# A second transform level on 64x32 and 32x64 tiles, eight in turn, in an attention and long-convolution kernel

## The chip, the cores and the metric

The kernel runs on one core of one Trainium2 chip, as one launch. TensorE (PE, with its weight loads as PEld), VectorE (DVE), ScalarE (ACT), GpSimd (POOL) and SyncE (SP) each work through a queue of their own, in order; DMA transfers run beside them on 16 DMA engines. The metric is the device time in microseconds (us). Before the change three runs took 217.52, 217.57 and 216.03 us, the median being 217.52.

## The reference

Two independent computations stand side by side in the output, 2048 positions by 2 x 576 columns, everything in bfloat16.

Half A is a sliding attention with 32 heads of 18 columns. Each position looks at 8 keys at distances 0, 2, ..., 14:

```python
qkv = (x @ wqkv).reshape(B, S, 3, H, Dh)          # H = 32, Dh = 18
idx = pos[:, None] - (jnp.arange(8) * 2)[None, :]
logits = einsum("bhsd,bhswd->bhsw", q, kg) * scale   # masked where idx < 0
o = einsum("bhsw,bhswd->bhsd", softmax(logits), vg)
a = o.reshape(B, S, D) @ wo
```

Half B is a gated long convolution. A four-tap filter along the positions, a product, a convolution as long as the sequence (by FFT in the reference), a direct term and another product:

```python
k_shift = sum(k_pad[:, t:t + S, :] * shift_k[:, 3 - t] for t in range(4))
kv = k_shift * v
y = irfft(rfft(kv, 2 * S) * rfft(ssm_k, 2 * S))[:S]
b = q * (y + kv * ssm_D)
```

## The kernel before

**The order** of all work is written out by hand in the string `ORDER` (lines 18 to 47). Each word names a step, its indices and, behind a colon, which PSUM pool it uses (`a` or `b`, two buffers of two banks each), which engine evacuates PSUM (`s` ScalarE, `v` VectorE) and which queue issues its DMAs (`c` ScalarE's; none means SyncE's). The loop at line 666 calls the steps in this order, and each engine's queue holds its instructions in it. Before the change no word has a `c`: every DMA is issued by SP. `MAP` (line 50) places all buffers in one arena of SBUF by hand, many of them sharing space one after another.

**DMA semaphores.** Eight of them go round in the order of issue, over all queues. A DMA therefore waits, in the queue that issues it, for the landing of the DMA eight issues earlier, and what stands behind it in that queue waits with it.

**Half A.** `xt` (line 364) loads x transposed by a DMA transpose, sixteen pieces in all; `xl4` and `x4` bring the last 64 columns. `qk` and `qt` (lines 391, 399) project queries and keys, `qt` those of the last 64 columns with weights that `wt` gathers; `v` (line 373) projects values. `lm` (line 495) multiplies queries by shifted keys on VectorE, `lb` (line 506) sums over the columns of a head on TensorE, `sm` (line 530) is the softmax. `pm` (line 598) multiplies values by weights, again on VectorE, 18 times; `ps` (line 604) sums over the eight keys. `po` (line 616) is the output projection: 72 matmuls on 32x128 tiles, two evacuations, and here one store per evacuation.

**Half B.** `lkn` loads the filter, `kt` and `kp` (lines 475, 485) transpose it and take the first transform level; `cv` (line 452) is the four-tap filter and the product with v, 32 VectorE operations; `sx` (line 464) takes the first level of kv. Both write the first level's result to scratch in DRAM (`Dk`, `Dx`), because the second level needs it with other indices on the partitions. `kl` and `xl` read it back, `ks` and `xs` do the second level through the helper `s2` (line 552), `gp` (line 575) multiplies the two spectra on VectorE, `gi` (line 583) is the inverse of the second level and writes to scratch `Dy`; `yl` reads that back, `ql` loads q, and `ys` (line 640) does the inverse of the first level, multiplies by q and stores. The second level's index runs over 32 blocks, four to a load (`i` from 0 to 7).

In `s2` a partition carries two interleaved residues. The weights `W2` hold, for each block, 64 columns in two halves, one for each residue; `tw` (line 345) makes them from the table `C2` by masks with zeros, so that a matmul with all 128 rows and 64 columns does both residues, half of it with zero weights. Two such tiles fill the array. `g_inv` uses 64 rows and 128 columns, also two tiles, with a table `IAt` that `ia` (line 410) makes from `W2` by transposes.

`evac` (line 117) is the copy from PSUM that most steps use, so most of ScalarE's work stands at line 119 and VectorE's copies at lines 121, 123 and 125.

Of the kernel before, what the change touches and what calls it, by code (L numbers as in the profile page):

```python
# [10 lines left out]
ALU = mybir.AluOpType  # L11
# [19 lines left out]
cv.3.7 sx.4.2:bs lb.2.0:bs ql.1 v.4:as sx.5.1:bs sx.5.2:bs v.3:as kl.3 sx.6.0:bs lm.3.0.0 lm.0.2.1 sx.6.1:bs v.1:as
kl.6 lb.3.0:bs ql.2 sx.7.0:as sx.6.2:as v.0:bs sx.7.1:as sx.7.2:as lm.0.1.1 lm.2.2.1 v.2:bs vh.0 sm.0.0 sm.0.1
lm.0.0.1 sm.0.2 sm.0.3 sm.0.4 lb.0.1:bs xl.3 v.5:as xl.6 lm.2.0.1 v.8:as lm.2.1.1 lb.2.1:bs vh.1 ks.6.0:as sm.0.5:b
ks.3.0:as ks.3.1:bs lm.1.0.1 lm.1.1.1 lm.3.1.1 kl.2 lb.1.1:av xs.3.0:bs ks.6.1:av xl.5 xs.3.1:bs xs.6.0:as sm.0.6 xl.2
xs.6.1:bs gp.3.0 gp.3.1 xl.4 v.7:as lm.3.0.1 v.6:as ks.2.0:bs xs.5.0:as vh.2 sm.0.7 gp.6.0 gp.6.1 lb.3.1:bs pm.0.2
ks.2.1:as xs.2.0:bv kl.5 pm.0.0 xs.2.1:as kl.4 lwo.3 xs.5.1:bs gi.3.0:as gi.6.0:bs pm.0.6 sm.1.0 gp.2.0 gi.3.1:as
sm.1.1 sm.1.2 ks.5.0:bs gp.2.1 ks.5.1:as sm.1.3 kl.1 ps.0.0:bs gp.5.0 ps.0.2:bs xl.1 xs.4.0:as xs.4.1:bs gi.6.1:as
gp.5.1 ks.4.0:bs ks.4.1:as kl.7 gi.5.0:bs pm.0.7 ps.0.6:as pm.0.1 ps.0.7:as ks.1.0:bv sm.1.4 ks.1.1:av xl.7 xs.1.0:bs
kl.0 gp.4.0 gi.5.1:as gp.4.1 gi.2.0:bs gi.2.1:as sm.1.5:b pm.0.4 gp.1.0 ks.7.0:as xs.1.1:bs xl.0 gi.4.0:av sm.1.6
pm.0.5 ql.7 gp.1.1 sm.1.7 gi.4.1:bs ks.7.1:as ps.0.1:bs gi.1.0:as xs.7.0:bs pm.0.3 ks.0.0:as gp.7.0 ps.0.4:bs lwo.2  # L40
gi.1.1:as ks.0.1:bs xs.7.1:av xs.0.0:bs gp.7.1 gp.0.0 xs.0.1:bs gp.0.1 lwo.1 gi.7.0:as gi.7.1:bs gi.0.0:as gi.0.1:bs
yl.3 yl.1 ps.0.5:as yl.2 pm.0.8 ps.0.3:as ps.0.8:bs po.0.1.1:s pm.1.7 pm.1.6 pm.1.1 ps.1.7:as po.0.1.0:s ps.1.1:as
yl.7 pm.1.2 ps.1.2:bs pm.1.5 ys.3.0:b ys.3.1:a po.0.0.1:s pm.1.3 ys.1.0:a ps.1.5:bs ys.1.1:a pm.1.0 yl.5 ps.1.6:bs
yl.6 ql.5 ys.2.0:a ys.2.1:b po.0.0.0:s ql.6 ps.1.0:bs yl.0 pm.1.4 pm.1.8 ps.1.3:bs ys.7.0:a ps.1.4:bs ys.7.1:a
ps.1.8:bs ql.0 ql.4 ys.5.0:b ys.5.1:a po.1.1.1:v yl.4 po.1.1.0:s ys.6.0:a ys.6.1:b ys.0.0:a ys.0.1:b po.1.0.1:v
po.1.0.0:s ys.4.0:a ys.4.1:b
# [4 lines left out]
    "C2": 0, "W2": 0, "c_i": 0, "vt1": 0, "lmask": 2048, "p_i": 2080, "sc_f": 2112, "ones1": 2144, "sc_i": 2272,  # L51
# [651 lines left out]
```

## Time and profile before

| | before |
|---|---|
| three runs | 217.52, 217.57, 216.03 us |
| profiled execution, its own time | 216.0 us |
| its span, first to last instruction | 214.2 us |
| DVE busy | 190.3 us (89%) |
| PE busy, weight loads | 185.7 us (87%), 113.3 us (53%) |
| ACT busy | 155.7 us (73%) |
| mean granted PE clock | 0.969 |
| DMA moved | 50.46 MB, mean 236 GB/s |

A row of a group names the line, the engine, the operation, output and input, the shapes and the count, then the busy time in us and the mean of one in ns, then how long the engine had been idle before such instructions and what ended the wait. A row of the timeline gives the start and the duration in us. `SPq` is SyncE's queue issuing DMAs. A DMA row gives the count, the size of one and the median time from issue to landing.

### The profile page before, as it was taken

To read this page: it belongs to the slowest core of one execution; us is meant where nothing else is said; L and a number is where in the kernel's file an instruction comes from. 1 tells how busy PE (TensorE), PEld (TensorE's weight loads), DVE (VectorE), ACT (ScalarE), POOL (GpSimd) and SP (SyncE) were. 2 spreads that over 40 slices of the span, in tenths; PEclk is the share of its full clock that TensorE was granted. 3 is DMA by queue.
4 is the path that set the end of the run, shared out by engine and by line. 5 is a ranking of instruction groups with operands and counts; after the bars stand their busy time and mean duration, and the time that the engine had idled before them with its cause. 6 is when DMAs were issued, how large, how long until landed. Compare 5 with 4: busy or idle time off the path is not lost.

```text
span 214.2 us, 6277 instructions
## 1 busy us (share of the span) xinstructions
PE 185.7 (87%) x2711; PEld 113.3 (53%) x2711; DVE 190.3 (89%) x174; ACT 155.7 (73%) x229; POOL 6.0 (3%) x24
## 2 busy tenths in 40 slices
PE   7389689999999999999969899879989988988760
PEld 2046345354343335556648567557656866756540
DVE  7777958999999999999999999999999998985432
ACT  3499599998969998887866999899999543340220
POOL 8200000000000000000000000000000000000000
PEclk9956999999999999999999999999999999999997
DMA  6999999999798898985748299767977399698693
GB/s 171 246 203 167 151 335 226 296 187 303 194 293 231 275 265 227 307 297 161 218 123 320 38 271 330 265 231 278 291 195 206 118 274 347 178 343 266 168 329 99
DMA packets 44874, 50.46 MB, mean 236 GB/s; under 512 B 16940, under 2 KB 37998, under 8 KB 44846
## 3 DMA queue, kind: packets, MB, share of 16 engines
q1 hardware_dynamic: 44846, 50.06, 84.3%
q8 instruction: 21, 0.34, 0.7%
q14 instruction: 7, 0.06, 0.1%
HBM read 28.94 MB, written 18.87 MB: 223 GB/s over the span
## 4 chain that ended last, share of the span: by engine, by line
DVE 50%; DMA 16%; PE 11%; issue 10%; SPq 8%; ACT 2%; DVEq 1%; ACTq 0%
DVE arena L500 13%; DVE arena L457 7%; DVE arena L602 7%; DVE arena L460 6%; DMA out_dram<-arena 5%; SPq L366 5%; DMA arena<-in_B_k_dram 5%; DVE arena L577 4%; DMA arena<-in_B_q_dram 3%; DMA arena<-in_B_ssm_k_dram 3%; PE psA L379 2%; ACT arena L119 2%; DVE arena L123 2%; DVE arena L462 2%; PE psB L623 2%
## 5 line engine op out<-in xcount | busy, mean ns | idle before, releaser
L119 ACT ACTIVATE arena<-psA 128x576 bf16<-128x576 f32 (+5 forms) x101 | 73.3, 764 | 32.9 <-PE psB L623 15.0
L119 ACT ACTIVATE arena<-psB 128x576 bf16<-128x576 f32 (+8 forms) x114 | 77.8, 720 | 14.5 <-PE psB L611 6.0
L602 DVE TENSOR_TENSOR arena<-arena 128x4096 bf16<-128x4096 bf16 x18 | 40.5, 2284 | 0.1
L500 DVE TENSOR_TENSOR arena<-arena 128x4096 bf16<-128x4096 bf16 x16 | 36.1, 2284 | 0.0
L371 PE MATMUL psA<-arena 128*128 128x512 bf16 x120 | 27.9, 379 | 2.5 <-DMA arena<-in_A_x_dram 2.0
L371 PEld LDWEIGHTS <-arena 128*128 128x128 bf16 x160 | 15.0, 98 | 20.7 <-issue 4.4
L457 DVE TENSOR_TENSOR arena<-arena 128x2304 bf16<-128x2304 bf16 x16 | 21.5, 1354 | 1.2 <-DMA arena<-in_B_k_dram 0.9
L577 DVE TENSOR_TENSOR arena<-arena 128x2304 bf16<-128x2304 bf16 x16 | 21.1, 1350 | 0.0
L557 PEld LDWEIGHTS <-arena 128*64 128x64 bf16 x256 | 13.8, 108 | 12.7 <-issue 11.9
L623 PE MATMUL psA<-arena 32*128 32x288 bf16 x288 | 19.7, 282 | 0.7 <-DVE arena L651 0.7
L623 PE MATMUL psB<-arena 32*128 32x288 bf16 x288 | 19.3, 281 | 1.0 <-issue 0.6
L623 PEld LDWEIGHTS <-arena 32*128 32x128 bf16 x576 | 15.9, 93 | 5.2 <-issue 3.5
L611 PEld LDWEIGHTS <-ident 64*64 64x64 bf16 x576 | 15.1, 106 | 5.4 <-issue 3.3
L379 PEld LDWEIGHTS <-arena 128*32 128x32 bf16 x360 | 14.5, 140 | 5.4 <-issue 1.4
L460 DVE TENSOR_TENSOR arena<-arena 128x2304 bf16<-128x2304 bf16 x12 | 16.3, 1354 | 0.4
L379 PE MATMUL psA<-arena 128*32 128x512 bf16 x280 | 16.2, 381 | 0.1
L590 PEld LDWEIGHTS <-arena 64*128 64x128 bf16 x256 | 12.7, 94 | 5.7 <-issue 2.2
L651 DVE TENSOR_TENSOR arena<-psA,arena 128x576 bf16<-128x576 f32 x10 | 7.4, 753 | 8.3 <-DMA out_dram<-arena 7.6
L557 PE MATMUL psB<-arena 128*64 128x288 bf16 x136 | 12.7, 290 | 1.9 <-DVE arena L125 0.9
L611 PE MATMUL psB<-arena,ident 64*64 64x256 bf16 x384 | 12.5, 271 | 1.7 <-DVE arena L602 1.2
L557 PE MATMUL psA<-arena 128*64 128x288 bf16 x120 | 12.0, 291 | 2.3 <-DVE arena L123 1.3
L590 PE MATMUL psA<-arena 64*128 64x288 bf16 x160 | 11.9, 283 | 0.5 <-DVE arena L125 0.2
(114 smaller groups left out, 195.5 us busy)
## 6 DMA issues: line engine op xcount, KB each, us to landing
Dk<-arena SPq DMA_DIRECT2D x8, 576.0 KB, 4.2
Dx<-arena SPq DMA_DIRECT2D x8, 576.0 KB, 4.4
arena<-Dk SPq DMA_DIRECT2D x8, 576.0 KB, 4.5
arena<-Dx SPq DMA_DIRECT2D x8, 576.0 KB, 5.2
Dy<-arena SPq DMA_DIRECT2D x8, 576.0 KB, 3.4
arena<-Dy SPq DMA_DIRECT2D x8, 576.0 KB, 4.5
out_dram<-arena SPq DMA_DIRECT2D x32, 144.0 KB, 4.3
arena<-in_A_wo_dram SPq DMA_DIRECT2D x4, 648.0 KB, 6.8
```

What stands on the lines that cost most here:

```text
L119: nc.scalar.activation(dst, src, ACT.Copy, **({} if scale is None else {"scale": scale}))
L371: nc.tensor.matmul(ps[:, u, :], w[:, kb, cols[u]:cols[u] + 128], xT[:, kb, t], start=(kb == 0), stop=(kb == 4))
L379: nc.tensor.matmul(ps[32 * a:32 * a + 32, u, :], wv[:, kb, 2 * n + u:D:DH], xv[kb][:, a], start=(kb == 0), stop=(kb == 4), tile_position=( ...
L457: nc.vector.tensor_tensor(tB() if k else tAr[c], kfull[:, 4 * c + 3 - j:4 * c + 7 - j, :], skb[:, j, :].unsqueeze(1).to_broadcast([128, 4, ...
L460: nc.vector.tensor_tensor(tAr[c], tAr[c], tB(), ALU.add)
L500: nc.vector.tensor_tensor(prr.get((m, h, hv)), qs[hv][h]().unsqueeze(1).to_broadcast([128, 2, 2, HS]), kv, ALU.mult)
L557: nc.tensor.matmul(ps[64 * hp:64 * hp + 64, im, 0:HD], W2[:, im, 4 * i + 2 * h + hp].rearrange("p l f -> p (l f)"), Wt[:, 2 * h + hp, d0:d ...
L577: nc.vector.tensor_tensor(P.rearrange("p (a b) d -> p a b d", a=2), X.unsqueeze(2).to_broadcast([128, 2, 2, D]), K.unsqueeze(1).to_broadca ...
L590: nc.tensor.matmul(ps[:, hp, 0:HD], IAt[r, tab, 2 * i + h, :], Pp[(i, h)][r, n, d0:d1], start=(n == 0), stop=(n == 3), tile_position=(64 * ...
L602: nc.vector.tensor_tensor(Pr.get((hv, p)), vv, Lt[hv]().unsqueeze(2).to_broadcast([128, W, 2, 256]), ALU.mult)
L611: nc.tensor.matmul(ps[64 * b:64 * b + 64, r, 0:256], ident[g, g], P[g, n, :, 128 * b:128 * b + 128], start=(n == 0), stop=(n == W - 1), ti ...
L623: nc.tensor.matmul(pss[e][:, b, 0:HD], Os[hv][g, d // 2, r, 128 * (d % 2):128 * (d % 2) + 128], wo4[g, d, d0:d1], start=(d == 0), stop=(d ...
```

## The change

The weights of the second level hold one residue each, without masks (`C2`, `lmask` and the step `tw` are gone), and a partition carries one residue: the lower 64 one, the upper 64 the other. `s2` takes 16 matmuls of 64 rows and 32 columns in one go, for two row groups and four column groups, on two PSUM buffers at once; its index `e` is a half of the 576 columns. `g_inv` takes 32 matmuls of 32 rows and 64 columns likewise. In both, two row groups write into one PSUM bank, on different partitions. The numbers of matmuls in `s2` and in `g_inv` go from 256 to 512 each.

The scratch `Dk`, `Dx`, `Dy` is laid out so that the first level's side sees 4608 bytes in a row and the second level's side 1152; before it was the other way round.

`po` puts both evacuations into one buffer and stores them by one DMA, eight stores in all where there were sixteen. The load of the first rows of k is cut into 48 and 15 partitions.

`ORDER` and `MAP` are new throughout. Some words now have a `c`: ACT's queue issues the filter loads, two of the sixteen transposes of x, some weight loads, half of the stores of `Dk` and `Dx`, one load from `Dk`, two stores and two loads of `Dy`, and some output stores. Twelve of the sixteen `ys` are evacuated by ScalarE, so that VectorE multiplies from SBUF; before all sixteen multiplied from PSUM.

```diff
-lkn.0 tj lkn.1 t2 t0 wm.11:b ib:bs t3 tv sh zw.1 lkn.2 lk.0 zw.0 sk.2:bv sk.0:bv lwq.0.1 t5 xl4 sk.1:bv xt.0.2 kt.7:av
+t1 sh:c t0 xl4 xt.0.0 lkn.1:c lkn.0:c tj lkn.2:c sk.1:as xt.1.2 t2 lwq.0.1 sk.0:as t3 zw.1 xt.0.3:c xt.1.3 tv sk.2:av
...
-ps.1.8:bs ql.0 ql.4 ys.5.0:b ys.5.1:a po.1.1.1:v yl.4 po.1.1.0:s ys.6.0:a ys.6.1:b ys.0.0:a ys.0.1:b po.1.0.1:v
-po.1.0.0:s ys.4.0:a ys.4.1:b
+ys.7.1:as yl.3 po.0.1.0:s ps.1.2:as ql.2 pm.1.7 yl.0:c ql.0 ys.6.0:av ys.6.1:bs ps.1.7:bs ys.2.0:as ql.3 ys.2.1:bs
+po.1.1.1:s po.1.1.0:v po.1.0.0:s ys.0.0:bv ys.0.1:as ys.3.0:bv ys.3.1:as po.1.0.1:sc
...
     def by_f1(Dd, i):
-        return Dd.rearrange("r f d -> f r d")[:, 4 * i:4 * i + 4, :]
+        return Dd.rearrange("h (q r) d -> (h q) r d", r=32)[:, 4 * i:4 * i + 4, :]
 
     def by_rt(Dd, i):
-        return Dd.rearrange("r (l h) d -> (r l) h d", h=32)[:, 4 * i:4 * i + 4, :]
+        return Dd.rearrange("h p d -> p h d")[:, 4 * i:4 * i + 4, :]
...
-    def t_w2():
-        for l in range(2):
-            evac(W2().rearrange("p i h l f -> p l (i h) f")[:, l], C2(), scale=lmask[:, l:l + 1])
...
-    def s2(Wt, i, dst, h, scale):
-        for e, (d0, d1) in enumerate(DCH):
-            ps = psb()
-            for im in range(2):
-                for hp in range(2):
-                    nc.tensor.matmul(ps[64 * hp:64 * hp + 64, im, 0:HD],
-                                     W2[:, im, 4 * i + 2 * h + hp].rearrange("p l f -> p (l f)"),
-                                     Wt[:, 2 * h + hp, d0:d1], start=True, stop=True, tile_position=(0, 64 * hp))
-            evac(dst[:, :, h, d0:d1], ps[:, :, 0:HD], scale=scale)
+    def s2(Wt, i, dst, e, scale):
+        pss = [psb(), psb()]
+        for im in range(2):
+            for hp in range(2):
+                for l in range(2):
+                    for h in range(2):
+                        o = 64 * (l ^ h) + 32 * hp
+                        nc.tensor.matmul(pss[h][o:o + 32, im, 0:HD], W2[64 * l:64 * l + 64, im, 4 * i + 2 * h + hp, :],
+                                         Wt[64 * l:64 * l + 64, 2 * h + hp, HD * e:HD * e + HD], start=True, stop=True,
+                                         tile_position=(64 * l, o))
+        for h in range(2):
+            evac(dst[:, :, e, HD * h:HD * h + HD], pss[h][:, :, 0:HD], scale=scale)
...
-    def g_inv(i, h):
-        Y = Yr[i] if h else Yr.get(i)
-        for d0, d1 in DCH:
-            ps = psb()
-            for n, tab in enumerate((0, 1, 1, 2)):
-                for hp in range(2):
-                    r = slice(64 * hp, 64 * hp + 64)
-                    nc.tensor.matmul(ps[:, hp, 0:HD], IAt[r, tab, 2 * i + h, :], Pp[(i, h)][r, n, d0:d1],
-                                     start=(n == 0), stop=(n == 3), tile_position=(64 * hp, 0))
-            evac(Y[:, 2 * h:2 * h + 2, d0:d1], ps[:, :, 0:HD])
+    def g_inv(i, e):
+        Y = Yr[i] if e else Yr.get(i)
+        P = Pp[(i, e)]
+        pss = [psb(), psb()]
+        for n, tab in enumerate((0, 1, 1, 2)):
+            for hp in range(2):
+                for b in range(2):
+                    for h in range(2):
+                        r, o = 64 * b + 32 * hp, 64 * (b ^ h)
+                        nc.tensor.matmul(pss[h][o:o + 64, hp, 0:HD], IAt[r:r + 32, tab, 2 * i + h, o:o + 64],
+                                         P[r:r + 32, n, HD * h:HD * h + HD], start=(n == 0), stop=(n == 3), tile_position=(r, o))
+        for h in range(2):
+            evac(Y[:, 2 * h:2 * h + 2, HD * e:HD * e + HD], pss[h][:, :, 0:HD])
...
+        stage = sAr.get((hv, r, di))
         for e in range(2):
-            stage = sAr.get((hv, r, di, e))
-            evac(stage, pss[e][:, :, 0:HD])
-            a = 8 * hv + 2 * (2 * r + e)
-            dq().dma_start(outt[:, a:a + 2, d0:d1], stage)
-            sAr.drop((hv, r, di, e))
+            evac(stage[:, 2 * e:2 * e + 2, :], pss[e][:, :, 0:HD])
+        a = 8 * hv + 4 * r
+        dq().dma_start(outt[:, a:a + 4, d0:d1], stage)
+        sAr.drop((hv, r, di))
```

More of the change, by code (lines that the diff above doesn't have):

```diff
@@ L315, in t_first @@
         nc.vector.tensor_copy(p_f(), p_i[:, 1:2])
-        nc.gpsimd.iota(g1(), pattern=[[4, 64]], base=1, channel_multiplier=0)
+        nc.gpsimd.iota(g1(), pattern=[[4, 32], [128, 2]], base=1, channel_multiplier=0)
         for ri in range(2):
-            nc.vector.tensor_scalar(n1[:, ri, :], g1(), p_f[:, 0:1], 64.0 * (1 + ri), op0=ALU.mult, op1=ALU.add)
+            nc.vector.tensor_scalar(n1[:, :, ri], g1(), p_f[:, 0:1], 64.0 * (1 + ri), op0=ALU.mult, op1=ALU.add)
         nc.vector.tensor_single_scalar(n1(), n1(), 255, ALU.bitwise_and)
-        nc.scalar.activation(T1(), n1(), ACT.Sin, bias=pib[:], scale=-2.0 * np.pi / 256)
+        nc.scalar.activation(T1(), n1().rearrange("p f r -> p (f r)"), ACT.Sin, bias=pib[:], scale=-2.0 * np.pi / 256)
     def t_second():
         nc.gpsimd.iota(g2(), pattern=[[4, 32], [256, 32]], base=0, channel_multiplier=0)
-        for i, bits in enumerate((1, 112, 4, 8, 2)):
+        for i, bits in enumerate((64, 28, 1, 2, 32)):
             nc.vector.tensor_single_scalar(sc_i[:, i:i + 1], p_i[:, 0:1], bits, ALU.bitwise_and)
@@ L339, in t_second @@
         nc.vector.tensor_single_scalar(n2(), n2(), 8191, ALU.bitwise_and)
-        nc.scalar.activation(C2().rearrange("p (i h) f -> p i h f", i=2), n2(), ACT.Sin, bias=pib[:], scale=-2.0 * np.pi / 8192)
+        nc.scalar.activation(W2(), n2(), ACT.Sin, bias=pib[:], scale=-2.0 * np.pi / 8192)
         nc.scalar.preload_act_table_set("natural_log_exp_and_others")
-        nc.vector.tensor_scalar(lmask[:, 0:1], sc_f[:, 0:1], -1.0, 1.0, op0=ALU.mult, op1=ALU.add)
-        nc.vector.tensor_copy(lmask[:, 1:2], sc_f[:, 0:1])
-    def t_w2():
-        for l in range(2):
-            evac(W2().rearrange("p i h l f -> p l (i h) f")[:, l], C2(), scale=lmask[:, l:l + 1])
     def t_heads():
@@ L421, in ib_table @@
         ptr = psum("b", 2, 1024, dt=BF16)
-        nc.tensor.transpose(ptr[:, 0, 0:64], T1[0:64].rearrange("p r f -> p (r f)"), ident[0:64, 0:64])
+        nc.tensor.transpose(ptr[:, 0, 0:64], T1[0:64], ident[0:64, 0:64])
         evac(IB(), ptr[:, 0, 0:64])
```

93 lines of the change are left out of this document (46 added, 47 removed), and 24 rows, old and new, of the table MAP.

## The prediction

> **What bounds the kernel now.** I read the page first, then the busy times by stage, then the timeline of the engine that is full.
>
> ```profile
> span 214.2 us, 6277 instructions
> ...
> PE 185.7 (87%) x2711; PEld 113.3 (53%) x2711; DVE 190.3 (89%) x174; ACT 155.7 (73%) x229; POOL 6.0 (3%) x24
> ...
> DVE 50%; DMA 16%; PE 11%; issue 10%; SPq 8%; ACT 2%; DVEq 1%; ACTq 0%
> ```
>
> DVE and PE look alike by share (89% and 87%), but the chain that ended last is half DVE and only 11% PE. I cut the span where the work of DVE changes: at 34.7 (the convolution runs), 87.7 (its last product), 120, 163.5 (last spectral product) and 190.4 (last attention product, step `pm`).
>
> ```profile
> 0.00:34.70 34.70, 26.09 (x177) 13.71 (x177) 26.12 (x48) 24.66 (x27) 5.66 (x23) 0.85 0.99 209
> 34.70:87.70 53.00, 51.61 (x399) 23.07 (x399) 52.42 (x40) 47.33 (x66) 0.33 (x1) 1.00 0.97 257
> 87.70:120.00 32.30, 29.76 (x473) 19.69 (x477) 32.23 (x23) 25.23 (x37) 0.00 (x0) 1.00 0.69 216
> 120.00:163.50 43.50, 39.74 (x632) 27.31 (x620) 43.43 (x37) 42.39 (x75) 0.00 (x0) 1.00 0.80 245
> 163.50:190.40 26.90, 24.61 (x688) 19.06 (x688) 26.17 (x18) 13.08 (x23) 0.00 (x0) 1.00 0.78 245
> 190.40:214.20 23.80, 13.84 (x352) 10.49 (x352) 9.93 (x15) 2.98 (x5) 0.00 (x0) 0.94 0.77 226
> ```
>
> Columns: stage, its length, busy PE, weight loads, DVE, ACT, POOL, granted PE clock, DMA share, GB/s. From 34.7 to 190.4 DVE is idle for 1.45 us in all. Before that it loses 8.58 us, while the DMA engines are full (0.99). So the span is DVE work up to the last `pm` (190.31 - 9.93 = 180.4), plus idle before it (8.58 + 1.45 = 10.0), plus a tail of 23.8 us in which no engine is full. Those are my three terms. ACT is second in the stage 120 to 163.5 (42.39 of 43.5); PE has 3.8 us to spare there.
>
> **Term 1, DVE work.** The changed program's instructions, counted engine by engine against the old ones, say which evacuations change engine. Prices:
>
> ```profile
> L651 DVE TENSOR_TENSOR arena<-psA,arena 128x576 bf16<-128x576 f32 x10 | 7.4, 753 | 8.3 <-DMA out_dram<-arena 7.6 <-PE psA L646 0.7
> ...
> L123 DVE CAST arena<-psA 128x576 bf16<-128x576 f32 x6 | 4.3, 752 | 0.4 <-issue 0.4
> ...
> L123 DVE CAST arena<-psB 128x1024 bf16<-128x1024 f32 x2 | 2.4, 1220 | 0.4 <-PE psB L448 0.4
> ...
> L123 DVE CAST arena<-psA 128x512 bf16<-128x512 f32 x1 | 0.7, 680 | 0.0
> ...
> L535 DVE TENSOR_TENSOR arena<-arena 128x512 bf16<-128x512 bf16 x2 | 0.8, 420 | 0.0
> ...
> L119 ACT ACTIVATE arena<-psA 128x576 bf16<-128x576 f32 x48 | 29.6, 673 | 21.5 <-PE psB L623 15.0 <-PE psA L623 6.1 <-PE psA L590 0.3
> ...
> L119 ACT ACTIVATE arena<-arena 128x2048 bf16<-128x2048 bf16 x2 | 3.9, 1998 | 0.0
> ```
>
> DVE evacuations of 576 columns fall from 19 to 12: -7 x 0.75 = -5.3. One of 1024 goes, one narrow 1024 and one 512-word copy come (about 0.68 each): +0.2. The tail projections `qt.0` and `qt.1` move to DVE, four 512-column casts of 0.68 and two of 16: +3.1. Twelve of the sixteen `y_step`s now let ACT evacuate and DVE multiply from SBUF; no row has 576 such columns, the 512 row (420 ns) scaled gives 0.45, bounds 0.42 and 0.75: 12 x (0.45 - 0.75) = -3.6. Four one-column table operations go, about -0.6. Sum -6.2: 190.3 becomes 184.1. After the last `pm` stand 5 products, 3 direct ones and 2 casts: 5 x 0.45 + 5 x 0.75 = 6.0, so 178.1 stands ahead of it, against 180.4.
>
> ACT loses the two masked copies of the twiddle table (-4.0) and gains 18 evacuations of 576 columns (12.1), the rest cancelling to about -3: 155.7 becomes some 161. Eight of those us lie in the last two stages, where ACT has 35 us free. In the spectral stage it gets two more steps, 2.4 us against 1.1 free; it can borrow from the stage before (7.1 free).
>
> **The tiles themselves.**
>
> ```profile
> 104.04 0.68 PE L557 MATMUL psA<-arena 128*64 128x288 bf16 x8
> ...
> 159.95 1.15 PE L590 MATMUL psA<-arena 64*128 64x288 bf16 x16
> ...
> 167.43 0.29 PE L623 MATMUL psA<-arena 32*128 32x288 bf16 x1
> ...
> 167.44 0.29 PE L623 MATMUL psB<-arena 32*128 32x288 bf16 x1
> ...
> 167.56 0.28 PE L623 MATMUL psA<-arena 32*128 32x288 bf16 x1
> ```
>
> Today `s2` (L557) and `g_inv` (L590) run two tiles at a time: 8 matmuls in 4 turns, 16 in 8. In L623 four tiles start within 0.01 us and the next four 0.12 us later; so a turn costs 0.12 us and the starts almost nothing. Each of the two steps has 256 matmuls in 128 turns now and 512 in 64 turns after: -128 x 0.12 = -15.4 us of PE. At worst starts fill the array no faster than four at a time, 0 saved. The value for the end is close to 0 either way: DVE is busy for 43.43 of 43.5 us where these steps run, and the two ACT evacuations behind a step (1.2 us) outlast its matmuls. What the new form costs: a step holds both buffers of its PSUM pool and its first evacuation waits for all 16 matmuls, which the other pool covers. I count 0, bounds -1 and +2.
>
> The row first: L623, L590 and L611 give every row group a bank of its own (`pss[e][:, b]`, `ps[:, hp]`). In the changed steps two row groups write one bank, in different partitions. The Trainium skill, page TensorEngine Tiling (Array Packing), section Gotcha 1: PSUM Pressure, says that different row tiles cannot use one PSUM bank at the same time; no row here shows such a pair. It makes the third rival.
>
> **Scratch layout.**
>
> ```profile
> Dk<-arena SPq DMA_DIRECT2D x8, 576.0 KB, 4.2
> arena<-Dk SPq DMA_DIRECT2D x8, 576.0 KB, 4.5
> ...
> Dy<-arena SPq DMA_DIRECT2D x8, 576.0 KB, 3.4
> arena<-Dy SPq DMA_DIRECT2D x8, 576.0 KB, 4.5
> ...
> arena<-in_A_wqkv_dram SPq DMA_DIRECT2D x2, 256.0 KB, 3.4
> ```
>
> Long and short pieces change sides: Dk and Dx are now written in 4608-byte pieces and read in 1152-byte ones, Dy the other way. The old Dk wrote short (4.2), the old Dy long (3.4); both reads take 4.5. Worth -0.8 on the way to the spectra and +0.8 on the way back: 0.
>
> **Term 2, idle before the last `pm`.** The start is built anew, with loads on ACT's queue too.
>
> ```profile
> SPq L366 <- DMA arena<-in_B_ssm_k_dram: 1.9, 1, 1.9
> ...
> L366 SPq DMA_TRANSPOSE arena<-in_A_x_dram x16: 1252/1274/10752, 6.8 to 52.9; - x16
> ...
> DMA to landing us min/median/max: 3.6/4.9/12.2
> ...
> 0.74 1.28 ACT L288 ACT_TABLE_LOAD   x1 [0.74 <-PEq L687]
> ...
> 3.41 0.87 DVE L326 CAST arena<-arena 128x5 f32<-128x5 int32 x1
> ...
> 8.64 2.00 ACT L340 ACTIVATE arena<-arena,pib 128x2048 bf16<-128x2048 int32 x1 [2.15 <-DVE arena L342]
> ```
>
> The first row is the rule of this program: eight DMA semaphores go round, so a DMA waits for the landing of the one eight issues before it, here a transpose for the first filter load. In the new order the second filter load, on ACT, waits so for `xl4` (256 KB; by the 256 KB row about 4.5 us), and behind it stand ACT's table load (1.28) and the first activation, for which L326 waits: 3.41 becomes about 6.2. From L326 to the table's sine took 5.2 us (3.41 to 8.64): sine at 11.4 to 13.4, second table load to 14.7, then the two transposes that are now ACT's (they also wait until SP's have landed), 2 x 1.27, to 17.3. Two evacuations (2 x 1.0), then `lwq.1.1` issued near 20 and landed near 23.7; `wt` 0.75, five matmuls 1.2, so `qt.0` is ready near 26. DVE has 23.2 us of work before the first convolution product in its new order (8.0 of tables, 15.2 of evacuations and `lm.*.2`); `qt.0`, `qt.1` and two `lm` take 5.5 from 26: 31.6, idle 8.4. With 1.6 for later loads I take 10.0 for the start (now 8.58); bounds 6 (all loads in time) and 17 (an ACT transpose that takes 10.75 us to issue, as the first one did). For the rest, 3.0 (now 1.45): 1.3 for ACT in the spectral stage and a little at the first `y_step`s, whose loads come just when five `pm` are done; bounds 1 and 7. Sum 13.0.
>
> Last `pm` at 178.1 + 13.0 = 191.1.
>
> **Term 3, the tail.**
>
> ```profile
> 190.38 1.42 DVE L651 TENSOR_TENSOR arena<-psA,arena 128x576 bf16<-128x576 f32 x2
> ...
> 210.10 1.26 SPq L654 DMA_DIRECT2D out_dram<-arena  x2
> ...
> DVE arena L651 <- DMA out_dram<-arena: 9.4, 4, 3.4
> ...
> 167.42 2.08 PEld L623 LDWEIGHTS <-arena 32*128 32x128 bf16 x72 [0.20 <-issue]
> ...
> 169.74 1.07 PE L611 MATMUL psA<-arena,ident 64*64 64x256 bf16 x32
> ...
> 175.75 0.44 PE L646 MATMUL psB<-arena 128*64 128x288 bf16 x4
> ```
>
> Today nine PE steps of the attention and four `y` pairs follow the last `pm`, and DVE stands 9.4 us for staging buffers still being stored. In the new order one `ps` (1.1), the pairs of tiles 6, 2, 0 and 3, and four `po` follow. On PE: `ps` (L611) 1.1, `ys.2` (two halves, L646) 0.8, three `po` (L623, 72 matmuls) at 2.2, four half `ys` at 0.4, one `po` 2.2, five PSUM handovers of 0.25 = 13.6. Then two evacuations (1.5) and one store, issue and landing 4.4 (the old end had 4.1 from the last product at 210.1 to 214.2): 19.5. Half as many attention stores, 8 for 16, save their issues (0.5 each) on SP, already in this. Bounds 17 and 24 (as now, if stagings wait again).
>
> **Sum.** 191.1 + 19.5 = 210.6, that is -3.6. The profiled execution took 216.0 for its span of 214.2, so 212.4. The three runs shown have 217.52 as median and 216.03 as lowest, so the profiled one is among the low ones; I lift the forecast a little for that: **213.0**.
>
> **Rivals.** (1) *Slower: ACT's queue starves the evacuations.* Eighteen DMAs stand in ACT's queue up to the loads of the spectra, nearly all waiting for a landing eight issues back, with evacuations behind them, and PE has only two buffers a pool. For: in the new order ACT's transposes wait for five landings; ACT was 47.33 of 53.0 busy in the convolution stage, so 5.7 us of waits there fill it. Against: SP bore such waits, and 16 scratch stores no longer block loads. Price: a transpose issue of 10.75 instead of 1.27 puts 9.5 us on the start, half a us for each of fourteen later issues 7; I take 8: 221. It decides from 6 us of lost DVE time beyond the 13.0. (2) *The start eats what the tail gives*: 4 us more idle, 217. For it: DMA is full for the first 87 us, and no bytes go away. (3) *Tiles take turns*: row groups sharing a bank go one after the other, so 4 tiles at a time as good as now, PE back at 185 with 32 more transposes; DVE hides most, +1.5: 214.5. By the skill's rule above this is the case. (4) *More*: idle falls to 8, tail 18: 206.
>
> **How the numbers follow.** Forecast 0.40 (209 to 215.3), rival 1 0.29, rival 2 0.13, rival 3 0.08, rival 4 0.10. One per cent (2.2 us) is about what this kernel's runs, 1.5 apart, can tell. Faster by over 1% (below 215.3): 0.40 + 0.10 + most of rival 3 = 0.56; within 1%: 0.14; slower: 0.30. Leaving a tenth on each side, the range is 206 to 221; the likeliest case alone spans 209 to 215.3.
>
> **What would show it.** After: DVE busy near 184; PE near 170 (185 if tiles take turns); a new `s2` step of 16 matmuls in about 0.45 us; last `pm` near 191 and 19.5 us behind it; first convolution product near 31. I am wrong if ACT idles on DMA landings for more than a few us, if DVE idles between 40 and 185, or if the last `pm` comes after 194.

## The result: 4% slower

The changed kernel takes 226.36 us (median), the kernel before 217.55 beside it: 1.0402 times as long, interval 1.0327 to 1.0477. The forecast was 213.0 (206 to 221). Some executions of every kernel are some per cent longer than its others: ratios leave them out as far as they could be told, a kernel with only one other execution (e7, e12, e13) has that one's time and no ratio, and the profiles of e1, e2, e7 and e10 to e14 are of such longer ones. The profiled execution took 225.12 us for a span of 223.3. The page of the changed kernel, the parts that were shown of the one before:

```profile
span 223.3 us, 7339 instructions
...
PE 182.0 (82%) x3247; PEld 105.1 (47%) x3255; DVE 185.6 (83%) x170; ACT 159.0 (71%) x239; POOL 5.6 (3%) x25
...
PE 49%; ACT 21%; DMA 16%; issue 7%; SPq 3%; ACTq 1%; DVE 1%
```

DVE has lost 4.7 us of work (6.2 were forecast), and yet the end is later: the chain that ended last, half DVE before, is now half PE and a fifth ACT. The same stretches as before, columns as before (length, PE, weight loads, DVE, ACT, POOL, granted PE clock, DMA share, GB/s):

```profile
0.00:34.70 34.70, 22.73 (x180) 12.13 (x183) 22.60 (x49) 16.43 (x18) 5.28 (x24) 1.00 0.86 201
34.70:87.70 53.00, 48.54 (x390) 23.82 (x396) 48.52 (x35) 42.22 (x56) 0.33 (x1) 0.97 0.84 222
87.70:120.00 32.30, 29.63 (x505) 16.53 (x502) 31.60 (x23) 28.07 (x39) 0.00 (x0) 1.00 0.74 235
120.00:163.50 43.50, 33.70 (x898) 17.76 (x891) 41.58 (x30) 39.42 (x71) 0.00 (x0) 0.92 0.77 225
163.50:190.40 26.90, 23.91 (x707) 17.22 (x710) 26.24 (x20) 18.97 (x35) 0.00 (x0) 0.94 0.83 254
```

DVE stands idle 12.1 us in the first row (8.6 before), 4.5 in the second (0.6), 3.3 in the other three (0.9). The last `pm` ends at 199.7 instead of 190.4, and the tail behind it is 23.6 us (23.8 before). In the terms of the forecast: work ahead of the last `pm` 179.8 (178.1 forecast), idle 19.9 (13.0), tail 23.6 (19.5). Work is 1.7 us off, idle 6.9, the tail 4.1.

**The start.** From the timeline of the changed kernel, ACT's queue, ACT and DVE:

```profile
1.32 6.60 ACTq L258 DMA_DIRECT2D arena<-in_B_ssm_k_dram  x2
...
7.95 1.28 ACT L287 ACT_TABLE_LOAD   x1 [7.95 <-DMA arena<-in_A_x_dram]
...
9.48 0.17 DVE L326 CAST arena<-arena 128x5 f32<-128x5 int32 x1 [4.38 <-ACT arena L287]
```

The second filter load stands in ACT's queue until `xl4` has landed; the table load and the first activation stand behind it, and DVE waits 4.38 us for them.

**The convolution stage.** The same view, 34.7 to 87.7:

```profile
77.46 0.81 ACT L118 ACTIVATE arena<-psB 128x768 bf16<-128x768 f32 x1 [2.45 <-DMA Dx<-arena]
...
78.32 3.89 PE L371 MATMUL psB<-arena 128*32 128x512 bf16 x40 [1.91 <-ACT arena L118]
...
83.52 2.29 DVE L493 TENSOR_TENSOR arena<-arena 128x4096 bf16<-128x4096 bf16 x1 [3.42 <-PE psB L514]
```

A store of `Dx` issued by ACT at 70.35 takes 7.0 us to land; an evacuation waits for its staging buffer, of which there are two, PE waits for the evacuation, and the product at L493 comes 3.42 us late. ACT's queue did not hold that store back for long:

```profile
L430 ACTq EVENT_SEMAPHORE  x7: 17/17/894, 23.3 to 102.7; - x7
...
DMA to landing us min/median/max: 2.8/3.7/7.0
```

L430 is the line of these stores; the waits ahead of those on ACT's queue lasted 0.89 us at most.

**The tail.** PE in the timeline, and two stretches behind it:

```profile
201.40 0.31 PE L645 MATMUL psB<-arena 128*64 128x288 bf16 x1 [1.28 <-issue]
...
208.42 0.29 PE L622 MATMUL psB<-arena 32*128 32x288 bf16 x1 [2.14 <-issue]
```

```profile
209.60:212.20 2.60, 2.60 (x52) 1.81 (x48) 0.59 (x2) 0.00 (x0) 0.00 (x0) 0.51 0.61 168
212.20:214.60 2.40, 2.40 (x71) 1.87 (x65) 0.96 (x2) 0.31 (x1) 0.00 (x0) 1.00 0.90 253
```

PE stands 2.14 us in the middle of a `po` with no releaser, and afterwards it is granted half its clock: 52 matmuls in 2.6 us, then 71 in 2.4. Another stop, of 1.28 us, lies at 201.4. DVE's longest wait in the tail is this one:

```profile
208.90 0.83 DVE L650 TENSOR_TENSOR arena<-arena 128x576 bf16<-128x576 bf16 x2 [6.01 <-DMA out_dram<-arena]
```

The row names a store; the products there also need q, whose loads stand late in SP's queue.

### The profile page after: what moved, and what is told of

Its sections match the earlier page's. It is cut to its first block, busy times and chain, and to the rows that moved or that the text cites. A ratio compares the mean times of both kernels' runs of the same rounds, so it can differ in the third digit from the quotient of the medians.

```text
span 223.3 us, 7339 instructions
## 1 busy us (share of the span) xinstructions
PE 182.0 (82%) x3247; PEld 105.1 (47%) x3255; DVE 185.6 (83%) x170; ACT 159.0 (71%) x239; POOL 5.6 (3%) x25
## 4 chain that ended last, share of the span: by engine, by line
PE 49%; ACT 21%; DMA 16%; issue 7%; SPq 3%; ACTq 1%; DVE 1%
ACT arena L118 20%; PE psB L363 7%; DMA Dx<-arena 6%; PE psA L371 5%; DMA arena<-in_A_wqkv_dram 5%; PE psB L622 4%; PE psA L610 3%; PE psB L610 3%; PE psA L363 3%; DMA arena<-Dy 3%; PE psA L622 3%; SPq L358 2%; DMA Dk<-arena 2%; PE psA L588 2%; PE psB L292 2%
## 5 line engine op out<-in xcount | busy, mean ns | idle before, releaser
L118 ACT ACTIVATE arena<-psA 128x576 bf16<-128x576 f32 (+4 forms) x114 | 81.6, 755 | 32.9 <-PE psA L622 7.3
L118 ACT ACTIVATE arena<-psB 128x576 bf16<-128x576 f32 (+7 forms) x113 | 78.3, 732 | 18.5 <-DMA Dx<-arena 3.5
L493 DVE TENSOR_TENSOR arena<-arena 128x4096 bf16<-128x4096 bf16 x16 | 36.4, 2286 | 3.5 <-PE psB L514 3.4
L363 PE MATMUL psB<-arena 128*128 128x512 bf16 x84 | 20.4, 379 | 1.7 <-ACT arena L118 1.2
L573 DVE TENSOR_TENSOR arena<-arena 128x2304 bf16<-128x2304 bf16 x16 | 21.3, 1353 | 0.0
L610 PEld LDWEIGHTS <-ident 64*64 64x64 bf16 x576 | 15.8, 111 | 4.2 <-issue 3.6
L552 PEld LDWEIGHTS <-arena 64*32 64x32 bf16 x512 | 7.2, 90 | 19.5 <-issue 18.4
L363 PE MATMUL psA<-arena 128*128 128x512 bf16 x68 | 16.2, 380 | 0.1
L588 PEld LDWEIGHTS <-arena 32*64 32x64 bf16 x512 | 9.0, 110 | 12.8 <-issue 10.4
L552 PE MATMUL psB<-arena 64*32 64x288 bf16 x288 | 12.3, 311 | 2.6 <-ACT arena L118 1.7
L588 PE MATMUL psA<-arena 32*64 32x288 bf16 x320 | 10.8, 315 | 4.4 <-issue 3.0
L552 PE MATMUL psA<-arena 64*32 64x288 bf16 x224 | 9.7, 298 | 4.1 <-ACT arena L118 3.3
L610 PE MATMUL psA<-arena,ident 64*64 64x256 bf16 x320 | 11.3, 285 | 0.3
```

The source lines that it names most:

```text
L118: nc.scalar.activation(dst, src, ACT.Copy, **({} if scale is None else {"scale": scale}))
L363: nc.tensor.matmul(ps[:, u, :], w[:, kb, cols[u]:cols[u] + 128], xT[:, kb, t], start=(kb == 0), stop=(kb == 4))
L493: nc.vector.tensor_tensor(prr.get((m, h, hv)), qs[hv][h]().unsqueeze(1).to_broadcast([128, 2, 2, HS]), kv, ALU.mult)
L552: nc.tensor.matmul(pss[h][o:o + 32, im, 0:HD], W2[64 * l:64 * l + 64, im, 4 * i + 2 * h + hp, :], Wt[64 * l:64 * l + 64, 2 * h + hp, HD * ...
L573: nc.vector.tensor_tensor(P.rearrange("p (a b) d -> p a b d", a=2), X.unsqueeze(2).to_broadcast([128, 2, 2, D]), K.unsqueeze(1).to_broadca ...
L588: nc.tensor.matmul(pss[h][o:o + 64, hp, 0:HD], IAt[r:r + 32, tab, 2 * i + h, o:o + 64], P[r:r + 32, n, HD * h:HD * h + HD], start=(n == 0) ...
```

## The experiments

My theories after the result: (a) ACT's queue, the prediction's first rival; (b) the table load alone; (c) a late q load in the tail; (d) the tiles themselves. The table sums up the runs in which they were tried. The times are medians of all executions. The idle columns are DVE's idle time in the profiled execution, in us: up to the end of the last convolution product (A), from there to the end of the last spectral product (B), and from there to the end of the last `pm` (C).

| kernel | us | ratio to before | idle A | idle B | idle C | tail |
|---|---|---|---|---|---|---|
| before | 217.6 | 1 | 9.2 | 0.1 | 0.7 | 23.8 |
| changed | 226.4 | 1.040 | 16.6 | 2.6 | 0.7 | 23.6 |
| e1 tiles only | 226.8 | 1.040 | 9.9 | 9.7 | 1.0 | 24.0 |
| e2 table load first | 232.1 | 1.072 | 21.3 | 6.1 | 2.8 | 21.8 |
| e3 all DMAs on SP | 221.6 | 1.025 | 11.5 | 2.5 | 2.2 | 23.0 |
| e4 q loads early | 227.0 | 1.045 | 16.0 | 4.2 | 2.7 | 22.1 |
| e5 e1, both pools | 228.6 | 1.056 | 10.9 | 7.6 | 4.8 | 21.7 |
| e6 e1, four in turn | 218.4 | 1.010 | 10.8 | 0.8 | 1.8 | 22.8 |
| e8 e3, four in turn | 219.1 | 1.015 | 11.6 | 0.6 | 1.8 | 20.3 |
| e17 e6, buffers held | 226.3 | 1.050 | 10.6 | 8.0 | 1.2 | 23.1 |

### ACT's queue, the table load, the tail

In e2 one word of the order moves:

```diff
-t1 sh:c t0 xl4 xt.0.0 lkn.1:c lkn.0:c tj lkn.2:c
+t1 tj sh:c t0 xl4 xt.0.0 lkn.1:c lkn.0:c lkn.2:c
```

> The changed kernel with one step moved: the first activation and its table load stand ahead of every DMA on ACT's queue. If the start loses its time to the table load that waits for a landing: the cast at L326 comes near 5 us instead of 9.5, the first convolution product near 31 instead of 34.6, and the whole falls by 2 to 4.4 us to 222 to 224. If the loads set the start anyway: the idle time only moves to the next wait on ACT's transposes and filters, first product still near 34, 226.

232.1 us, ratio 1.0717 (1.0648 to 1.0786): worse, as neither side had said. The table load ran at 0.74, but ACT's queue found its next wait:

```profile
23.30 2.54 ACTq L358 DMA_TRANSPOSE arena<-in_A_x_dram  x2
25.89 1.02 ACT L118 ACTIVATE arena<-psB 128x1024 bf16<-128x1024 bf16 x1 [9.25 <-DMA arena<-in_B_k_dram]
```

With its first wait gone, ACT's queue met other semaphores of the eight: its two transposes now stood behind a transpose on SP that took 12.0 us to land and a load of k (those land after 9 to 13 us here), and an evacuation stood 9.25 us behind them. The wait was moved, not removed.

In e3 every `c` is dropped from the order, so that SP issues all DMAs:

```diff
-t1 sh:c t0 xl4 xt.0.0 lkn.1:c lkn.0:c tj lkn.2:c
+t1 sh t0 xl4 xt.0.0 lkn.1 lkn.0 tj lkn.2
...
```

> The changed kernel with every DMA issued by SP, none by ACT. If ACT's queue starves the evacuations (first rival of the prediction): ACT no longer idles on landings ahead of its evacuations, DVE idle ahead of the last pm falls from 20 to 13 or less, 218 to 221 us. If the landings are late wherever they are issued: within 2 us of 226, or slower, because SP now bears the waits of all and the stores and loads stand behind one another.

221.6 us, ratio 1.0254 (1.0185 to 1.0322), 4.7 us less than the changed kernel by the medians, and the intervals of the two ratios don't meet. Its first two stretches:

```profile
0.00:34.70 34.70, 26.00 (x195) 13.45 (x196) 23.98 (x50) 16.99 (x19) 5.27 (x24) 0.95 0.87 201
34.70:87.70 53.00, 50.98 (x457) 23.90 (x456) 52.25 (x37) 46.80 (x61) 0.33 (x1) 1.00 0.88 241
```

DVE idles 10.7 and 0.75 us where it was 12.1 and 4.5. So issuing DMAs from ACT costs the convolution stage 3.7 us and the start 1.4. In the convolution stage the way is not the one that the first rival describes, evacuations behind a DMA that waits in ACT's queue: the evacuation waited for a staging buffer whose store took 7.0 us to land, and in e3 the slowest of these stores took 4.9. Why it landed later is not shown. Idle in e3 up to the last `pm` is 16.2, not the 13 that was expected.

In e4 the q loads of tiles 2, 0 and 3 move up on SP:

```diff
-pm.1.1 ql.7 ps.1.5:as
+pm.1.1 ql.7 ql.2 ps.1.5:as
...
-ys.1.1:as ps.1.1:as
+ys.1.1:as ql.0 ps.1.1:as
...
-ys.7.1:as yl.3
+ys.7.1:as ql.3 yl.3
```

> The changed kernel with the loads of q tiles 2, 0 and 3 moved ahead on SP to the place where their buffers come free. If the tail is long because a q load stands late in SP's queue: the 6.0 us in which DVE stands at L650 go to 1.5 or less, and the tail falls from 23.6 to 19 to 20.5, the whole to 222 to 223.5. If staging buffers or PE set the tail: the gap at L650 stays or turns into one of the same size on a store, 226.

227.0 us, ratio 1.0447 (1.0361 to 1.0533), nothing gained. The wait of 6.0 us is gone, but the products that had waited now run ahead of the last `pm` or wait for PE, one of DVE's evacuations 4.5 us: the tail is 22.1 us, the last `pm` 3.7 later. So DVE stood there for a q load, and that set nothing.

### The tiles alone

e1 is the kernel before with the new `s2`, `g_inv`, tables, scratch layout and load of k in two pieces, with the old order (without `tw`), the old memory map and the sixteen small attention stores.

```diff
-t1 sh:c t0 xl4 xt.0.0 lkn.1:c lkn.0:c tj lkn.2:c
+lkn.0 tj lkn.1 t2 t0 wm.11:b ib:bs t3 tv sh
...
-    Wr, sAr = ring("W", 4, 4, D), ring("sA", 3, 4, HD)
+    Wr, sAr = ring("W", 4, 4, D), ring("sA", 5, 2, HD)
```

> The small tiles, the tables they need and the new scratch layout, with the steps in the order of the kernel before (without the masked table copies) and its sixteen small attention stores. If the loss comes from the new order of the steps: 215 to 218 us, DVE idle ahead of the last pm near 10 us as before, tail near 24. If the tiles or the layout cost something themselves (both PSUM buffers of a pool held by one step, a lower granted clock, later landings of the scratch stores): 220 to 226 us, with DVE idle of 3 us or more between 120 and 190 or ACT waiting for Dx stores between 35 and 88.

226.8 us, ratio 1.0399 (1.0293 to 1.0505): by itself the form of the tiles costs as much as the whole change. Up to the last convolution product DVE idles hardly more than before, so the layout costs nothing there; in the spectral stage (column B) it loses 9.7 us, and between 120 and 163.5 the granted clock is 0.76 (over the whole kernel 0.90 to 0.92 in its four executions, 0.95 to 0.96 in those of the kernel before):

```profile
120.00:163.50 43.50, 34.54 (x850) 20.12 (x845) 34.94 (x29) 34.72 (x60) 0.00 (x0) 0.76 0.67 201
```

PE, ACT and DVE all have time to spare there. From the same kernel's timeline:

```profile
120.41 0.28 PE L553 MATMUL psA<-arena 64*32 64x288 bf16 x1
...
121.34 0.43 PE L553 MATMUL psA<-arena 64*32 64x288 bf16 x15 [0.65 <-ACT arena L119]
...
122.25 1.22 ACT L119 ACTIVATE arena<-psA 128x576 bf16<-128x576 f32 x2
...
141.14 1.36 DVE L574 TENSOR_TENSOR arena<-arena 128x2304 bf16<-128x2304 bf16 x1 [4.62 <-PE psA L589]
```

A step starts one matmul, then waits until the second buffer of the pool has been evacuated, runs its other 15, and only then has ACT something to evacuate. Two suspects follow: the step that owns both buffers and hands them over at its end, or the sparser PE and its lower clock. In e5 a step takes one buffer of each pool, in e6 one after the other:

```diff
-        pss = [psb(), psb()]
+        pss = [pool.tile([128, 2, 512], FP32, name=n) for pool, n in ((pa, "psA"), (pb, "psB"))]
```

```diff
-        pss = [psb(), psb()]
-        for im in range(2):
+        for h in range(2):
+            ps = psb()
+            for im in range(2):
...
+            evac(dst[:, :, e, HD * h:HD * h + HD], ps[:, :, 0:HD], scale=scale)
```

> The kernel of the run with the tiles alone (old order of the steps), with one edit: a step of s2 or g_inv takes one PSUM buffer of each of the two pools instead of both buffers of one. Still eight tiles in turn. If that run lost its time because a step must wait until both evacuations of the step before it are done: the 8.0 us of DVE idle between the last convolution product and the last spectral product fall to 2 or less, granted clock back over 0.9 between 120 and 163.5, 216 to 219 us. If the sparser use of PE lowers the clock by itself: the clock stays near 0.75 there and the time at 222 or more.

> The same kernel with the other remedy: small tiles, but the loop over the two PSUM buffers outermost, so that four tiles run in turn, a buffer is taken only when its half starts, and its evacuation begins after half of the matmuls. PE works twice as long on these steps as with eight in turn. If holding both buffers is the cost: 215 to 218 us, idle as in the kernel before (0.7 to 2 us in the spectral stage). If small tiles or the layout cost by themselves: 222 or more, as with eight in turn.

e5 takes 228.6 us (1.048 to 1.063): no help. e6 takes 218.4, ratio 1.0103 (1.0051 to 1.0155): four tiles in turn give back three of the four per cent, with the same tiles, layout and number of matmuls. Its spectral stage:

```profile
120.00:163.50 43.50, 36.13 (x1004) 20.66 (x1011) 42.79 (x36) 41.77 (x74) 0.00 (x0) 1.00 0.80 238
```

That leaves the clock open: it is steady with four in turn alone, and e5, at 0.96 in this stretch, still has some of 4 us and more at 0.57 to 0.61 (112 to 120, 136 to 140, 188 to 192, cut into pieces of 4 us). Three kinds of run were meant to tell it from the buffers. First, every matmul of `s2` and `g_inv` issued twice, to keep PE busy, on e5 (e9) and on e1 (e10):

```diff
-        for im in range(2):
+        for im in (0, 1, 0, 1):
...
-        for n, tab in enumerate((0, 1, 1, 2)):
+        for n, tab in 2 * tuple(enumerate((0, 1, 1, 2))):
```

> Old order of the steps, eight tiles in turn, a buffer of each pool, as in the run of 228.6 us, and now every matmul of s2 and g_inv is issued twice with the same result, the second time over the first. Nothing else changes; PE has about 15 us more to do. If the loss comes from the lower granted clock that PE gets when it has less to do: no stretch of 4 us between 88 and 190 under a clock of 0.9, the DVE waits of 1.9, 3.7 and 4.3 us behind such stretches gone, and the time falls to 217 to 221 us although more is computed. If the clock is only a companion of the waits: 228 to 233 us.

> The run with the tiles alone (both buffers of one pool), with every matmul of s2 and g_inv issued twice. If the clock is the whole loss: 217 to 221 us, as with a buffer of each pool. If holding both buffers of a pool costs by itself beside the clock: clock back near 1.0 between 120 and 163.5, but ACT still short of work there and 222 to 226 us.

247.4 and 247.1 us, far beyond every expectation, with 24 us of idle DVE in the spectral stage though PE is not full there. From the weight loads of the first of them:

```profile
135.65 0.42 PEld L589 LDWEIGHTS <-arena 32*64 32x64 bf16 x17 [4.34 <-issue]
...
146.38 0.26 PEld L589 LDWEIGHTS <-arena 32*64 32x64 bf16 x17 [2.04 <-issue]
...
156.30 0.72 PEld L553 LDWEIGHTS <-arena 64*32 64x32 bf16 x49 [2.31 <-issue]
```

PE stops in the middle of a step with no releaser. Counted along PE's instructions, the stops of 1.4 us and more between 130 and 225 come at numbers 3257, 3769, 4281, 5305, 5561, 6329 and 7865: all multiples of 256 apart. At each of them a packet of 16 KB of the instruction queue is under way: it begins between 1.1 us ahead of the stop and 1.6 behind its start, takes about 1 us, and PE goes on 1.3 to 1.5 us behind its end. I read these as waits for PE's code; the two runs tell nothing of the clock. The changed kernel's stops at 147.7, 201.4 and 208.4 come at numbers 3257, 5817 and 6073, again multiples of 256 apart, so by the same reading the two stops in its tail are waits for code too.

Then fillers: at the end of each step four matmuls of 224 columns into PSUM columns that nobody reads, on e5 (e13) and on e1 (e14).

```diff
+        for p in pss:
+            for bk in range(2):
+                nc.tensor.matmul(p[:, bk, HD:512], ident[:], IAt().rearrange("p a v t -> p (a v t)")[:, 0:512 - HD], start=True, stop=True)
```

> Old order of the steps, eight tiles in turn, a buffer of each pool (the run of 228.6 us), with four filler matmuls of 224 columns at the end of each step of s2 and g_inv, into PSUM columns that nobody reads: 192 matmuls, some 18 us of PE work, but only 384 instructions. If eight in turn loses because the sparse PE is given a lower clock: the clock stays over 0.95 between 110 and 195 and the time falls to 219 to 223 us though PE does more. If the two-pool form loses for another reason: 228 or more.

> The same fillers in the run with the tiles alone (both buffers of one pool, 223 to 227 us). If the clock is the whole loss there: 218 to 221 us. If a step that holds both buffers costs by itself: clock over 0.95, but DVE still idle for 4 us or more in the spectral stage and 222 or more, and more than the two-pool form with fillers.

223.9 us (e13) and 228.5 (e14, ratio 1.0489, 1.0406 to 1.0573). The spectral stage of e13:

```profile
120.00:163.50 43.50, 41.98 (x1012) 24.45 (x1004) 38.77 (x32) 36.59 (x63) 0.00 (x0) 1.00 0.71 210
```

The clock is at full and DVE still idles 4.7 us of it; in e14 it is at full there too, and DVE idles 5.4. The fillers aren't free, though: evacuations waited for them too, so the clock falls as the sole cause, not as a helper.

Last, e17: four tiles in turn as in e6, but the matmuls ordered so that a step owns both buffers from its first matmul on and finishes both with its last two.

```diff
-        for h in range(2):
-            ps = psb()
+        pss = [psb(), psb()]
...
+        for h, im, hp, l in seq[1][:1] + seq[0][:7] + seq[1][1:7] + seq[0][7:] + seq[1][7:]:
```

> Small tiles in the old order of the steps, four in turn as in the run of 218.4 us, but the matmuls of a step ordered so that it must own both buffers of its pool from its first matmul on and finishes both with its last two. PE works as long as with four in turn. If owning both buffers and the late evacuation are the cost of eight in turn: 223 us or more, DVE idle of 4 us or more between the last convolution product and the last spectral product, the granted clock staying over 0.95 or not. If the sparser PE and its clock are the cost: 217 to 220 us, idle under 2 us.

226.3 us, ratio 1.050 (1.029 to 1.0711), and 8.0 us of idle DVE in the spectral stage, with a clock of 0.88 in this stretch:

```profile
120.00:163.50 43.50, 33.89 (x891) 19.92 (x881) 36.90 (x30) 35.96 (x63) 0.00 (x0) 0.88 0.70 208
```

With PE's work as in e6, owning both buffers and evacuating late brings the loss back, and the low clock with it. That is the cost of eight in turn here; that one pool or two makes no difference (e5) fits the late evacuation better than the number of buffers, but the two weren't tried apart.

### Both remedies on the changed kernel

The edits are those shown: e7 is e3 with a buffer of each pool, e8 e3 with four in turn, e11 the changed kernel with four in turn and ACT's queue left as it is, e12 e8 with the early q loads.

> The changed kernel with all DMAs on SP and a step of s2 or g_inv taking one buffer of each pool. If holding both buffers of a pool still costs in the new order of the steps: the 2.5 + 2.1 us of DVE idle from the last convolution product to the last pm fall to 2, and the time from 221.6 to 218 to 219.5. If the new order already covers it: 221 to 222.

> The changed kernel with all DMAs on SP and the two PSUM buffers of a step one after the other, four tiles in turn. As in the run with both pools: 218 to 219.5 if the buffers still cost in the new order, 221 to 222 if not. If eight tiles in turn are worth PE time to the whole, this one is slower than that one by 1 us or more.

> The changed kernel, ACT's DMAs as they are, with the two PSUM buffers of a step one after the other, four tiles in turn. With all DMAs on SP this edit went from 221.6 to about 219. If the two losses (ACT's queue, eight in turn) are independent: 226.4 - 2.5 to 4 = 222.5 to 224. If ACT's queue alone holds the changed kernel back: 226.

> All DMAs on SP, four tiles in turn, and the q loads of tiles 2, 0 and 3 issued as soon as their buffers are free. With the clock steady the tail of that kernel still has a DVE wait of 6.0 us for a q load: if that wait is the tail's bound, 219.1 falls by 2 to 4 to 215 to 217; if PE and the stores behind it are, 219.

e7 takes 218.4 us, e8 219.1 (four executions from 215.9 to 221.0; ratio 1.0149, 1.0075 to 1.0223), e11 226.5 (1.0342, 1.0219 to 1.0465), e12 218.3. So of the 4.0% of the changed kernel, issuing from ACT makes about 1.5 (against e3), and the buffers about 1 more by the ratios (e3 against e8, whose intervals overlap; e11 against the changed kernel doesn't resolve it). The 1.5% that e8's ratio leaves is not assigned to a cause; its profiled execution, the fastest, took 215.9, no more than the kernel before. Up to the first convolution product DVE idles 12.1 to 17.3 us in the four kernels of the new order that issue from ACT, and 10.5 to 11.0 in the four that don't. e12 again shows nothing from the q loads.

### The tail, and PE's code

e15 is the kernel before with four staging buffers for the last products, the two new ones where `K0` was; e16 has the changed kernel's longer attention stores as well.

```diff
-    qtr, ysr = ring("qt", 4, 2, D), ring("ys", 2, 2, D)
+    qtr, ysr = ring("qt", 4, 2, D), ring("ys", 4, 2, D)
```

> The kernel before with four staging buffers for the last products instead of two, in space that is free by then. DVE stands 9.4 us there for staging buffers still being stored. If those waits set the tail: 216.4 falls by 3 to 6 to 210.5 to 213.5. If the queue of SP and PE stand right behind: within 1.5 us of before.

> The same with the attention results stored in larger pieces as well (8 stores instead of 16, three staging buffers of twice the size). If fewer issues on SP help the tail as the prediction had it: 1 to 3 us below the run with four staging buffers alone. If a store that waits for two evacuations is later by as much: the same within 1 us.

216.2 us, ratio 0.997 (0.9921 to 1.002), and 216.0, ratio 0.9949 (0.9905 to 0.9993). DVE's waits for staging, 9.4 us before, are gone in both, and the time is the same within 1%: behind them stands PE, as in this row of e15's timeline.

```profile
199.77 0.76 DVE L651 TENSOR_TENSOR arena<-psA,arena 128x576 bf16<-128x576 f32 x1 [1.87 <-PE psA L646]
```

The longer stores add 0.2 us by the medians, which is within the noise. No kernel here has a lower median than e16.

e18 adds 512 matmuls of 8 columns to the kernel before, to price four more blocks of PE code:

```diff
+            for k in range(4):
+                r, b = divmod(k % 4, 2)
+                g = slice(64 * r, 64 * r + 64)
+                nc.tensor.matmul(ps[64 * b:64 * b + 64, r, HD:HD + 8], ident[g, g], ident[g, 0:8], start=True, stop=True, tile_position=(64 * r, 64 * b))
             evac(dst[:, :, h, d0:d1], ps[:, :, 0:HD], scale=scale)
```

> The kernel before with 512 matmuls of 8 columns added to the steps s2 and g_inv, into PSUM columns that nobody reads: four blocks of PE code more, as the small tiles bring, and about 5 us of PE time. If PE's code loads cost by themselves: 2 to 5 us more than before, with PE standing 1 us or more, with no releaser, at instruction numbers 256 apart. If not: within 1 us of before.

227.4 us, ratio 1.062 (1.0368 to 1.0872), but the question isn't answered: the small matmuls cost PE 15.8 us, not 5, and PE is full in the spectral stage.

```profile
120.00:163.50 43.50, 43.50 (x880) 25.46 (x880) 38.49 (x31) 38.21 (x64) 0.00 (x0) 1.00 0.70 215
```

No stop of PE over 1 us lies there. What four more blocks cost by themselves stays open.

## Why the prediction was wrong

The span came out 12.7 us over the 210.6 of the sum. Of these, 4.8 lie in term 2's rest, where the convolution stage was given nothing; 4.1 in the tail; 2.1 in the start; 1.7 in DVE's work ahead of the last `pm`.

**Term 1, DVE work:** near. 185.6 us against 184.1 forecast; the multiplications from SBUF took 0.45 us, as scaled.

**"What the new form costs ... I count 0, bounds -1 and +2":** a step that failed, and in the old order the dearest, though the changed kernel shows little of it. In the old order the form costs 9.7 us of idle DVE in the spectral stage (0.1 before) and three of the four per cent (e1 against e6, e17). I had seen both of its features, the two buffers and the first evacuation behind 16 matmuls, and believed that the other pool covers them; e5 shows that even a buffer of each pool doesn't. The new order covers most of it (2.6 us of idle) and pays in the first 95 us instead.

**Term 2, the start:** 10.0 forecast, 12.1 measured up to 34.7. The mechanism was as told; the landing of `xl4` took 6.8 us instead of 4.5, so L326 came at 9.48 instead of 6.2.

**Term 2, the rest:** 3.0 forecast, 7.8 measured. I gave the convolution stage nothing and it lost 4.5 up to 87.7, 3.7 of it to the DMAs that ACT issues (e3). Rival 1 named the queue, the place (ACT's spare 5.7 us) and the point of decision, 6 us beyond the 13.0; 6.9 came. Its way holds for the start, where the table load stood behind a filter load that waited for `xl4`; in the convolution stage it was a staging buffer whose store landed late, so that rival 1 comes near there is partly luck. Its price of 8 us was above the 4.7 that e3 gives back.

**Term 3, the tail:** 19.5 forecast, 23.6 measured. The PE work was rightly added up; two stops of PE with no releaser (1.28 us at 201.4 and 2.14 at 208.4, read above as waits for code) and the half clock after the second weren't in it. That these make the 4.1 us is argued, not shown by a run of its own. In e8's profiled execution, with stops of 1.1 and 1.2 us there and the clock at 1.00 in the tail, the three terms come to 179.7 + 14.0 + 20.3 = 214.0. The 9.4 us of staging waits, which the forecast of the tail counted as avoidable, were worth next to nothing by themselves (e15).

**The tiles** (rival 3): false.

```profile
138.15 0.44 PE L552 MATMUL psA<-arena 64*32 64x288 bf16 x16
```

Sixteen matmuls in 0.44 us, 0.45 forecast; the rule of the Trainium skill, page TensorEngine Tiling (Array Packing), section Gotcha 1: PSUM Pressure, that row tiles cannot use one bank at once, doesn't hold for such pairs on different partitions. But the saving of 15.4 us of PE was mis-sized:

```profile
L552 PE MATMUL psB<-arena 64*32 64x288 bf16 x288 | 12.3, 311 | 2.6 <-ACT arena L118 1.7 <-DVE arena L122 0.4
L588 PE MATMUL psA<-arena 32*64 32x288 bf16 x320 | 10.8, 315 | 4.4 <-issue 3.0 <-ACT arena L118 1.1
L552 PE MATMUL psA<-arena 64*32 64x288 bf16 x224 | 9.7, 298 | 4.1 <-ACT arena L118 3.3 <-DVE arena L122 0.3
...
L588 PE MATMUL psB<-arena 32*64 32x288 bf16 x192 | 5.8, 312 | 2.0 <-ACT arena L118 1.8
```

The four rows make 38.6 us, those of the kernel before 43.6: 5.0 saved. A short step is mostly the 0.3 us that one matmul takes to pass, and some ran at half clock. That the saving would be worth nothing at the end was right: four in turn, without it, makes the faster kernel (e6 against e1).

**Scratch layout:** 0 was right for the stage of the stores (e1: 9.9 us of idle against 9.2).

## What to carry to other kernels

Before packing a step more densely, ask when its first result can be evacuated and when its buffers come back: finishing everything at once turns a stream into a stop and go, and the engine that evacuates pays. A queue that also carries evacuations should not issue DMAs that may wait for landings; removing the first such wait only brings up the next. A wait that disappears from a tail proves nothing until it is seen what the same instruction waits for then.

## What I had not expected of the hardware

PE seems to wait for its own code where it consumes it fast. In the changed kernel it stops in the middle of a `g_inv`:

```profile
147.74 0.92 PE L588 MATMUL psA<-arena 32*64 32x288 bf16 x17 [3.02 <-issue]
...
149.22 1.22 PE L552 MATMUL psA<-arena 64*32 64x288 bf16 x16
```

A 16 KB packet of the instruction queue began at 145.1 and took 1.0. The page of the profile counts 21 such packets before and 25 after, about one for 256 of PE's matmuls and weight loads. The Trainium skill, page Runtime: NRT & Kernel Launch, section Instruction fetch mechanics, calls crossing such a border mostly hidden; here the stops of 1.3 to 4.3 us at borders of 256 say that it isn't always.

Behind the longer of these stops PE is granted half its clock for some microseconds: 0.51 in the stretch after the stop at 208.4, and in the changed kernel's spectral stage, behind the stop at 147.7, 16 matmuls took 1.22 us that take 0.44 otherwise.
